# Linear attention on one core: the store of head 13 as three transfers of 76, 48 and 4 partitions

## Chip, cores, metric

One core of one Trainium2 chip runs the kernel. The metric is the device time of one execution in microseconds; before the change it is 171.12 us, the median of three runs (171.07, 171.12, 171.43).

## What is computed

For each of 32 heads, with q, k and v of 2048 x 128 in bf16 and φ(x) = x + 1 for x > 0, exp(x) otherwise:

```python
def reference(q, k, v):
    phi_q = jnp.where(q > 0, q + 1, jnp.exp(q)) + 1e-6
    phi_k = jnp.where(k > 0, k + 1, jnp.exp(k)) + 1e-6
    kv = jnp.einsum("bhsd,bhse->bhde", phi_k, v)
    z = jnp.einsum("bhsd->bhd", phi_k)
    num = jnp.einsum("bhqd,bhde->bhqe", phi_q, kv)
    den = jnp.einsum("bhqd,bhd->bhq", phi_q, z)[..., None] + 1e-6
    return num / den
```

So each head loads three tensors of 512 KB and stores one of 512 KB; 64 MB move in all.

## The kernel before

The work of a head is laid out as 128 partitions (p) by 16 tiles (j) of 128 columns. Row p of a head's tensor in HBM, as `rows` (L228) takes it, is the 16 x 128 elements that belong to partition p: 4 KB without a gap. A load or store of a head is one transfer of 128 such rows.

Per head: SP loads k, q and v (L281). φ is taken as min(exp(x), 1) + 1e-6 plus max(x, 0), in two parts that TensorE adds up. ACT makes exp(k) (L289), DVE min and add (L295), POOL the max (L291) and, for five of 16 tiles, the sum of the two (L300). PE multiplies both with v into kvz_ps (L316), with a column for z (L319). PE transposes q (L335), ACT and DVE make φ of it (L346, L349, L352, L355). PE multiplies φ(q) with kv and z (L370, L371); DVE adds 1e-6 to the denominators (L415), inverts them (L419) and multiplies into o_sb (L391, L397). For the last three heads ACT takes a part of that (L406). SP stores o_sb (L431).

The order is written out by hand. `Plan` (L20) collects every operation with its engine and a due key; each engine's stream is its operations sorted by key. `Plan.emit` (L60) finds which semaphore values each operation has to wait for (L111, L112) and issues it (L113). At the end of SP's stream stand waits for every store's semaphore (L121).

Buffers: six for each of k, v and q (NBI, L158), ten for o_sb (NBO, L159). A load of head h has key h - 6.8 to h - 7.95, so loads run about six heads ahead. A store of head h has key h + 1 + 0.18 h (`late`, L435): the later the head, the further behind its computation the store is issued, so that loads go first, and the stores that are left follow when the last load has been issued. Store 13 has key 16.34, and follows the load of v for head 23. All of these, save the load of v for head 0 (ACT, L276), are issued by SP, in one queue. The semaphores of the stores are one for each o_sb buffer, and three more for the pieces in which the stores of heads 30 and 31 go out (PIECES and EXTRA, L181, L182): two and three groups of tiles, each over all 128 partitions.

Of the kernel before, what the change touches and what calls it, by code (L numbers as in the profile page):

```python
# [144 lines left out]
def bass_standalone__linear_attn_elu__prompt_kernel(  # L145
# [8 lines left out]
    NT = 16  # L154
# [3 lines left out]
    NBI = 6  # L158
    NBO = 10  # L159
# [20 lines left out]

    PIECES = {NH - 2: ((0, 6), (6, NT)), NH - 1: ((0, 6), (6, 12), (12, NT))}  # L181
    EXTRA = {NH - 2: 0, NH - 1: 1}  # L182

    qf = q.rearrange("b h s d -> (b h) s d")
    kf = k.rearrange("b h s d -> (b h) s d")
    vf = v.rearrange("b h s d -> (b h) s d")
    of = out.rearrange("b h s d -> (b h) s d")

    with ExitStack() as es:
        def sb(name, shape, dt):  # L190
            return es.enter_context(nc.sbuf_tensor(name, shape, dt))
# [14 lines left out]
        o_sb = sb("o_sb", [P, NBO, NT, D], bf16)  # L206
# [11 lines left out]
        def dma_sem(name):  # L218
            return dsems[name]

        for n, c in (("k", NBI), ("q", NBI), ("v", NBI), ("o", NBO + 3), ("x", 1)):
            for i in range(c):
                dsems[(n, i)] = es.enter_context(nc.semaphore(f"s_{n}{i}"))

        block = es.enter_context(nc.Block())
        pl = Plan()

        def rows(x, h):  # L228
            return x[h].rearrange("(p j) d -> p (j d)", j=NT)
# [7 lines left out]
               reads=[("id0",)], writes=[("ident",)])  # L237
# [29 lines left out]
        for h in range(NH):  # L267
# [3 lines left out]
            bi, b2, b3, bo = h % NBI, h % 2, h % 3, h % NBO  # L271

            def load(name, buf, src, key, h=h, bi=bi):
# [4 lines left out]
                if name == "v":  # L278
# [11 lines left out]
                   reads=[("k", bi)], writes=[("ek", b2)])  # L290
            pl.add("pool", h, lambda g, bi=bi, b3=b3: g.tensor_scalar(rk_sb[:, b3, :], k_sb[:, bi, :], BIG, 0.0,  # L291
                                                                      op0=ALU.min, op1=ALU.max),
                   reads=[("k", bi)] + ([("emq", 1)] if h == 2 else []), writes=[("rk", b3), ("rkx", b3), ("phik", b3)])
            pl.add("dve", at("emk", -3 + 0.95),
                   lambda d, b2=b2, b3=b3: d.tensor_scalar(emk_sb[:, b3, :], ek_sb[:, b2, :], 1.0, EPS, op0=ALU.min, op1=ALU.add),  # L295
                   reads=[("ek", b2)], writes=[("emk", b3)])

            def added(x, b3=b3):
# [3 lines left out]
                reads=[("emk", b3), ("rkx", b3)] + ([("emq", (h - 1) % 3)] if h else []), writes=[("phik", b3)])  # L302

            def kv(pe, tiles, srcs, h=h, bi=bi, b3=b3):
                for j in tiles:
# [17 lines left out]
                   reads=[("emk", b3), ("rk", b3), ("v", bi), ("ones",), ("vones",)], writes=[("bankkv",)])  # L323
            pl.add("pe", at("kv", -1.2), lambda pe, kv=kv: kv(pe, ADD, (rk_sb,)), reads=[("phik", b3), ("v", bi)], writes=[("bankkv",)])
            pl.add("act", at("kvs", -0.95), lambda a, b3=b3: a.activation(kvs_sb[:, b3, 1:], kvz_ps[:, 1:NC], ACT.Copy),
                   reads=[("bankkv",)], writes=[("kvs", b3)])
            pl.add("dve", at("zs", -1 + 0.905), lambda d, b3=b3: d.tensor_scalar(  # L327
                kvs_sb[:, b3, 0:1], kvz_ps[:, 0:1], kvz_ps[:, NC:NC + 1], None, op0=ALU.add),
                   reads=[("bankkv",)], writes=[("zs", b3)])
# [14 lines left out]
            for half in (0, 1):  # L344
                pl.add("act", h - 1.1 + 0.05 * half,
                       lambda a, b2=b2, c=cols(half): a.activation(eq_sb[:, b2, c], xT_ps[:, c], ACT.Exp),  # L346
                       reads=[("bankx", half)], writes=[("eq", b2, half)])
            pl.add("act", h - 1.0,
                   lambda a, b3=b3, c=cols(1): a.activation(rq_sb[:, b3, c], xT_ps[:, c], ACT.Relu),  # L349
                   reads=[("bankx", 1)], writes=[("rq", b3, 1)])  # L350
            pl.add("dve", at("rq", -2 + 0.948),
                   lambda d, b3=b3, c=cols(0): d.tensor_scalar(rq_sb[:, b3, c], xT_ps[:, c], 0.0, None, op0=ALU.max),  # L352
                   reads=[("bankx", 0)], writes=[("rq", b3, 0)])
            pl.add("dve", at("emq", -2 + 0.955),
                   lambda d, b2=b2, b3=b3: d.tensor_scalar(emq_sb[:, b3, :], eq_sb[:, b2, :], 1.0, EPS, op0=ALU.min, op1=ALU.add),  # L355
                   reads=[("eq", b2, 0), ("eq", b2, 1)], writes=[("emq", b3)])
# [4 lines left out]
            def nbank(b, h=h):  # L361
                return ("bankx", b) if h == NH - 1 and b < 2 else ("banko", b)
# [48 lines left out]
            for g, (b0, b1, place_d, runs) in enumerate(groups):  # L411
# [6 lines left out]
                    reads=banks, writes=[("den", b3, g)])  # L418
                pl.add("dve", key + 0.01, lambda d, b3=b3, b0=b0, b1=b1: d.reciprocal(  # L419
                    rden_sb[:, b3, 4 * b0:4 * b1], den_sb[:, b3, 4 * b0:4 * b1]),  # L420
                    reads=[("den", b3, g)], writes=[("rden", b3, g)])
                if g == 0:
                    pl.add("dve", h + 0.911, last_tile, reads=[nbank(0), nbank(1), ("rden", b3, 0)], writes=[("o", bo, NT - 1)])
                for n, (eng, t0, t1, *place_a) in enumerate(runs):
                    pl.add(eng, h + place_a[0] if eng == "act" else key + 0.012 + 0.004 * n,
                           div_act(t0, t1) if eng == "act" else div(t0, t1),
                           reads=[nbank(b) for b in range(t0 // 3, (t1 + 2) // 3)] + [("rden", b3, g)],
                           writes=[("o", bo, t) for t in range(t0, t1)])

            def store(t0, t1, key, slot, h=h, bo=bo):  # L430
                pl.add("sp", key, lambda sp: sp.dma_start(rows(of, h)[:, t0 * D:t1 * D],  # L431
                                                          o_sb[:, bo, t0:t1].rearrange("p j d -> p (j d)")),
                       reads=[("o", bo, t) for t in range(t0, t1)], dma=("o", slot))

            late = h + 1.0 + 0.18 * h  # L435
            for n, (t0, t1) in enumerate(PIECES.get(h, ((0, NT),))):
                store(t0, t1, late + 0.01 * n, bo if n == 0 else NBO + EXTRA[h] + n - 1)

# [29 lines left out]
```

## Time and profile before

| | |
|---|---|
| time, median of 3 | 171.12 us |
| profiled execution | 171.33 us |
| its span, first to last instruction | 169.5 us |
| mean granted TensorE clock | 0.988 |
| busy PE / PEld / DVE / ACT / POOL | 93% / 92% / 89% / 93% / 62% |
| HBM read / written | 50.33 MB / 16.78 MB, 396 GB/s over the span |

How to read the profile. The page gives the busy share of each engine, then the span in 40 slices, each digit a share in tenths. The row "DMA" is the mean busy share of the core's 16 DMA engines, and the lines on queues give packets, MB and their share of the 16 engines' time: q1 is the queue that SP feeds, q10 that of ACT, q8 and q14 fetch instructions. The chain of work follows the computing instruction that ended last back through what released it. The same DMA rows can be asked for any stretch of the span, again in 40 slices. A line on the issues of one source line gives the time from issue to landing. Behind that stand the landing marks: each transfer raises its semaphore in 16 steps, and the trace has the time of each; a transfer has landed with its last.

The tail of the span, in numbers: the last load is issued at 141.14 us, the last store at 164.41; DVE's last instruction starts at 163.04.

### The profile page before, as it was taken

What the parts mean: (1) busy time and instruction counts of PE and PEld (TensorE: products, weight loads), DVE (VectorE), ACT (ScalarE), POOL (GpSimd) and SP (SyncE); (2) the same over time, 40 slices, a digit from 0 to 9 for tenths busy, and PEclk for the clock granted to TensorE, in tenths of its full rate; (3) what the DMA queues carried; (4) which work ended last, traced back from release to release, by engine and by line L of the source; (5) the groups of instructions that cost most, each with busy time, mean ns of one, the idle gap of its engine ahead of it and who ended that gap; (6) DMA issues with size and microseconds to landing.
All of it is one profiled execution on the core that took longest, in us unless ns stands there. A gap on an engine that the chain in (4) does not pass through costs nothing.

```text
span 169.5 us, 7127 instructions
## 1 busy us (share of the span) xinstructions
PE 157.0 (93%) x3116; PEld 155.6 (92%) x3116; DVE 150.1 (89%) x293; ACT 157.5 (93%) x180; POOL 105.6 (62%) x72
## 2 busy tenths in 40 slices
PE   7559999999999999999999999999999999999920
PEld 7559999999999999999999999999999999999820
DVE  0164999999999999999999999999999999999860
ACT  4699999999999999999999999999999999996950
POOL 3837776666666777666666777666666677755000
PEclk9999999999999999999999999999999999999995
DMA  5999999999999999999999999999999999999984
GB/s 209 407 416 410 412 408 403 399 406 414 414 405 410 417 411 411 414 411 411 410 414 412 410 414 412 409 423 407 413 418 408 409 416 412 410 418 412 411 344 174
DMA packets 22862, 67.56 MB, mean 399 GB/s; under 512 B 2096, under 2 KB 2608, under 8 KB 22832
## 3 DMA queue, kind: packets, MB, share of 16 engines
q1 hardware_dynamic: 22688, 66.59, 98.6%
q8 instruction: 24, 0.39, 0.9%
q10 hardware_dynamic: 144, 0.52, 0.8%
q14 instruction: 6, 0.05, 0.1%
HBM read 50.33 MB, written 16.78 MB: 396 GB/s over the span
## 4 chain that ended last, share of the span: by engine, by line
PE 87%; DMA 3%; DVE 3%; ACT 3%; issue 0%; SPq 0%
PE kvz_ps L316 36%; PE o_ps L370 17%; PE o_ps L371 17%; PE x_ps L335 16%; DMA q_sb<-in_q_dram 3%; DVE o_sb L397 1%; ACT eq_sb L346 1%; PE kvz_ps L319 1%; ACT ek_sb L289 1%; ACT rq_sb L349 1%; DVE emk_sb L295 0%; DVE rden_sb L419 0%; DVE den_sb L415 0%; SPq L281 0%; DVE o_sb L391 0%
## 5 line engine op out<-in xcount | busy, mean ns | idle before, releaser
L300 POOL TENSOR_TENSOR rk_sb<-rk_sb,emk_sb 128x640 bf16<-128x640 bf16 x32 | 44.7, 1398 | 47.3 <-DVE emq_sb L355 41.6
L346 ACT ACTIVATE eq_sb<-x_ps 128x1024 bf16<-128x1024 bf16 x64 | 70.1, 1276 | 3.2 <-PE x_ps L335 3.1
L289 ACT ACTIVATE ek_sb<-k_sb 128x2048 bf16<-128x2048 bf16 x32 | 70.1, 2190 | 1.8 <-DMA k_sb<-in_k_dram 1.8
L397 DVE TENSOR_TENSOR o_sb<-o_ps,rden_sb 128x768 bf16<-128x768 f32 (+2 forms) x63 | 68.0, 1120 | 0.1
L316 PE MATMUL kvz_ps<-v_sb,rk_sb 128*128 128x128 bf16 (+1 forms) x512 | 67.2, 218 | 0.0
L291 POOL TENSOR_SCALAR rk_sb<-k_sb 128x2048 bf16<-128x2048 bf16 x32 | 60.6, 1895 | 2.7 <-DMA k_sb<-in_k_dram 2.0
L370 PE MATMUL o_ps<-kvs_sb,emq_sb 128*128 128x129 bf16 (+1 forms) x536 | 61.1, 217 | 0.3 <-DVE o_sb L397 0.3
L371 PE MATMUL o_ps<-kvs_sb,rq_sb 128*128 128x129 bf16 (+1 forms) x536 | 61.1, 217 | 0.0
L316 PE MATMUL kvz_ps<-v_sb,emk_sb 128*128 128x128 bf16 (+1 forms) x352 | 54.9, 218 | 2.3 <-DVE kvs_sb L327 2.1
L319 PE MATMUL kvz_ps<-ones_sb,rk_sb 128*128 128x1 bf16 x388 | 53.1, 165 | 0.0
L370 PEld LDWEIGHTS o_ps<-kvs_sb,emq_sb 128*128 128x128 bf16 x536 | 50.6, 98 | 0.6 <-DVE o_sb L397 0.4
L371 PEld LDWEIGHTS o_ps<-kvs_sb,rq_sb 128*128 128x128 bf16 x536 | 50.1, 97 | 0.0
L316 PEld LDWEIGHTS kvz_ps<-v_sb,rk_sb 128*128 128x128 bf16 x512 | 46.8, 97 | 0.0
L349 ACT ACTIVATE rq_sb<-x_ps 128x1024 bf16<-128x1024 bf16 x32 | 41.2, 1289 | 0.0
L319 PE MATMUL kvz_ps<-ones_sb,emk_sb 128*128 128x1 bf16 x228 | 37.6, 166 | 0.0
L316 PEld LDWEIGHTS kvz_ps<-v_sb,emk_sb 128*128 128x128 bf16 x352 | 33.5, 97 | 2.8 <-issue 2.4
L335 PE MATMUL x_ps<-ident,q_sb 128*128 128x128 bf16 x512 | 33.8, 219 | 1.7 <-DMA q_sb<-in_q_dram 1.7
L319 PEld LDWEIGHTS kvz_ps<-ones_sb,rk_sb 128*128 128x128 bf16 x388 | 35.4, 96 | 0.0
L335 PEld LDWEIGHTS x_ps<-ident,q_sb 128*128 128x128 bf16 x512 | 29.9, 98 | 2.0 <-DMA q_sb<-in_q_dram 2.0
L295 DVE TENSOR_SCALAR emk_sb<-ek_sb 128x2048 bf16<-128x2048 bf16 x32 | 21.9, 686 | 8.3 <-ACT ek_sb L289 8.3
L352 DVE TENSOR_SCALAR rq_sb<-x_ps 128x1024 bf16<-128x1024 bf16 x32 | 21.9, 683 | 2.0 <-ACT eq_sb L346 2.0
L355 DVE TENSOR_SCALAR emq_sb<-eq_sb 128x2048 bf16<-128x2048 bf16 x32 | 22.8, 712 | 0.4 <-ACT eq_sb L346 0.4
(28 smaller groups left out, 90.8 us busy)
## 6 DMA issues: line engine op xcount, KB each, us to landing
k_sb<-in_k_dram SPq DMA_DIRECT2D x32, 512.0 KB, 13.2
q_sb<-in_q_dram SPq DMA_DIRECT2D x32, 512.0 KB, 13.2
v_sb<-in_v_dram SPq DMA_DIRECT2D x31, 512.0 KB, 13.7
out_dram<-o_sb SPq DMA_DIRECT2D x30, 512.0 KB, 13.7
out_dram<-o_sb SPq DMA_DIRECT2D x3, 192.0 KB, 5.2
v_sb<-in_v_dram ACTq DMA_DIRECT2D x1, 512.0 KB, 4.3
out_dram<-o_sb SPq DMA_DIRECT2D x1, 320.0 KB, 6.1
out_dram<-o_sb SPq DMA_DIRECT2D x1, 128.0 KB, 4.6
```

Of the source, the lines that this page charges most:

```text
L289: lambda a, bi=bi, b2=b2: a.activation(ek_sb[:, b2, :], k_sb[:, bi, :], ACT.Exp),
L291: pl.add("pool", h, lambda g, bi=bi, b3=b3: g.tensor_scalar(rk_sb[:, b3, :], k_sb[:, bi, :], BIG, 0.0, op0=ALU.min, op1=ALU.max), reads=[( ...
L300: pl.add("pool", h + 0.5, lambda g, added=added: g.tensor_tensor(out=added(rk_sb), in0=added(rk_sb), in1=added(emk_sb), op=ALU.add), reads ...
L316: last = pe.matmul(kvz_ps[:, 1 - l:NC + r], lhsT=w, rhs=rhs, start=first, stop=fin, skip_group_check=True)
L319: last = pe.matmul(kvz_ps[:, z:z + 1], lhsT=w, rhs=ones_sb[:, 0:1], start=False, stop=fin, skip_group_check=True)
L335: last = pe.transpose(xT_ps[:, j * P:(j + 1) * P], q_sb[:, bi, j * P:(j + 1) * P], ident[:])
L346: lambda a, b2=b2, c=cols(half): a.activation(eq_sb[:, b2, c], xT_ps[:, c], ACT.Exp),
L349: lambda a, b3=b3, c=cols(1): a.activation(rq_sb[:, b3, c], xT_ps[:, c], ACT.Relu),
L355: lambda d, b2=b2, b3=b3: d.tensor_scalar(emq_sb[:, b3, :], eq_sb[:, b2, :], 1.0, EPS, op0=ALU.min, op1=ALU.add),
L370: pe.matmul(o_ap, lhsT=emq_sb[:, b3, t * P:(t + 1) * P], rhs=kvs_sb[:, b3, c0:c1], start=True, stop=False)
L371: return pe.matmul(o_ap, lhsT=rq_sb[:, b3, t * P:(t + 1) * P], rhs=kvs_sb[:, b3, c0:c1], start=False, stop=True)
L397: return lambda d: d.tensor_tensor(out=o_sb[:, bo, t0:t1, :].rearrange("p (a b) d -> p a b d", b=n), in0=_ap(nfull(b), 512 * b + NC * (t0 ...
```

## The change

The store of head 13 no longer goes out as one transfer of 128 partitions of 4 KB, but as three: partitions 0 to 75, 76 to 123 and 124 to 127, each with all 16 tiles. They take the place of the one store in SP's order, at keys 16.34, 16.35 and 16.36. The first keeps the semaphore of its o_sb buffer; the other two get semaphores of their own, for which two are added. Nothing else is changed: no other transfer, no computation, no buffer.

```diff
     EXTRA = {NH - 2: 0, NH - 1: 1}
+    UNEVEN = 13
...
-        for n, c in (("k", NBI), ("q", NBI), ("v", NBI), ("o", NBO + 3), ("x", 1)):
+        for n, c in (("k", NBI), ("q", NBI), ("v", NBI), ("o", NBO + 5), ("x", 1)):
...
             late = h + 1.0 + 0.18 * h
+
+
+            if h == UNEVEN:
+                r0 = 0
+                for n, r in enumerate((76, 48, 4)):
+                    pl.add("sp", late + 0.01 * n, lambda sp, h=h, bo=bo, r0=r0, r=r: sp.dma_start(
+                        rows(of, h)[r0:r0 + r, :], o_sb[r0:r0 + r, bo].rearrange("p j d -> p (j d)")),
+                        reads=[("o", bo, t) for t in range(NT)], dma=("o", bo if n == 0 else NBO + 2 + n))
+                    r0 += r
+                continue
             for n, (t0, t1) in enumerate(PIECES.get(h, ((0, NT),))):
```

## Prediction

> **What bounds the kernel now.** I read the page from the top: the engines' shares, the slices, the DMA queues, the chain.
>
> ```profile
> DMA  5999999999999999999999999999999999999984
> ...
> q1 hardware_dynamic: 22688, 66.59, 98.6%
> ...
> q8 instruction: 24, 0.39, 0.9%
> ...
> PE 87%; DMA 3%; DVE 3%; ACT 3%; issue 0%; SPq 0%
> ```
>
> The chain says PE, 87%. But it follows computing instructions only, and the last of these, L397 of head 31, starts at 163.04 and takes 0.96 us, so it ends at 164.0, while the span is 169.5. The other lines say what fills those 5.5 us: the 16 DMA engines are full from the second slice to the end, nearly all of it queue q1, which SP feeds. So I ask for the DMA view of the last 4.2 us (165.3 to 169.5, 40 slices of 0.105 us), and for SP's waits:
>
> ```profile
> DMA  9799866555655565556566566422110000000000
> ...
> q1 hardware_dynamic: 505, 0.71, 44.9%
> ```
>
> ```profile
> SPq L121 <- DMA out_dram<-o_sb: 3.9, 5, 1.2
> ```
>
> All 16 engines work until about 165.9. From 166.0 to 167.8 the row stays at 5 to 6 tenths: about 9 of 16 engines work and 7 have nothing left. The last row moves near 168.4. SP's last instructions (L121) wait 3.9 us for just these landings. **The end is set by the nine engines that are behind, not by the sum of the traffic.**
>
> The landing marks say the same. Every transfer leaves 16, one per engine (131 transfers, 2096 marks). The first and the last of one transfer lie 0.5 us apart at 11 us, 2.2 at 40, 3.7 at 80, 5.1 from 119 on. For store 28 (landing 160.03 to 165.12) six engines land within 0.76 us of the first, a seventh 2.2 us after it, the other nine 4.4 to 5.1 after it. What holds an engine back is visible: the 24 instruction packets of q8, 16 KB each, are 0.9% of 16 x 169.5 us = 24.4 us, or 1.0 us of one engine each. The gaps between landing marks show eight engines hit three times each (24 in all), every hit costing 1.3 to 1.6 us, and a ninth falling back slowly. The seven others never meet one. The last store is issued at 164.41; its idle engines land at 166.1 to 166.3, its last mark comes at 169.0. Store 13 is issued at 103.25 and needs 13.8 us to land, with the queue full:
>
> ```profile
> L431 SPq DMA_DIRECT2D out_dram<-o_sb x1: 873/873/873, 103.3 to 103.3; - x1
> ...
> DMA to landing us min/median/max: 13.8/13.8/13.8
> ```
>
> **The change part by part.**
>
> *The shares.* One row of one store is 4 KB. A 128-row transfer is 8 rows on each of 16 engines. Successive marks of one engine lie 1.245 us apart for such a transfer, so a row costs 0.156 us (413 GB/s in the stretch 120 to 140 us, over 16, gives 0.159). The trace shows no other row count. If the shares stay equal, as in all 131 transfers, 48 rows are 3 on each of 16; 76 = 4 x 19 can be dealt equally to 4, 2 or 1 engines at most; 4 rows to 4. I take four: it uses the most engines that equal shares allow, so it is nearest to the row seen. Then four engines carry 19 + 3 + 1 = 23 rows in place of 8, if the 4-row piece goes to the same four: **15 more, +2.34 us**. The other twelve carry 3 in place of 8: **5 fewer, -0.78 us**. The bounds: uneven shares on all 16 change nothing; one engine for all 76 gets 76 + 3 to 4 - 8, about 71.5 rows, or +11.1 us.
>
> *Which four.* No packet record names its engine. If all four are among the seven that finish early: the nine finish 0.78 us earlier, with 5.08 - 0.78 = 4.30 us behind the first. Of the four, an engine that was up to 0.76 behind comes to 3.10, under 4.30. The seventh, 2.22 behind, would come to 2.22 + 2.34 = 4.56 and would then be last: 4.56 - 5.08 = **-0.52 us**. Without it the gain is the whole **-0.78 us**. By count, four out of seven include it 4 times in 7. So -0.52 is the likelier of the two.
>
> For the four being early ones I have one hint. Packets of one engine follow each other at 155 ns, exact to 1 ns over long stretches, so engines can be followed by their phase. Records that start in the same nanosecond keep the order of the table they came from. Of 776 such pairs 619 fit one order of the engines, in which four of the early seven stand ahead of every engine that fetches (one against two of these: 29 to 0 and 21 to 0). Two more early ones stand in the middle, one at the very end. Whether that table runs by number, or as text does (0, 1, 10, 11, ..., 15, 2, 3, ...), the numbers 0 to 3 fall on early engines. It is a hint, since 157 pairs do not fit.
>
> *Page and row.* On the four, the Trainium skill ("DMA: Bandwidth & Descriptors", section "Why a DMA increments its semaphore by 16 and not by 1") says that a transfer from SP uses the largest count up to 16 that divides the rows, on the lowest-numbered engines: 76 on four, 48 on 16, 4 on four. No run here shows this; it would give the same +15 and -5 rows on engines 0 to 3. Against the change speaks the same page's section "Rules for kernel authors": coalesce small transfers, use one 128-partition transfer. With the page's fixed cost of about 2 us per transfer (a fit for another issuing path) two more would be +4 us if nothing hid them, 175.1; the row of 13.8 us to landing, some ten transfers deep, says they are hidden.
>
> *Two more issues on SP.* The 35 issues of L431 take 0.33 to 3.22 us, median 1.08, most of it waiting for room in the queue. Two more cost 0.66 to 2.2 us of SP. Behind them wait the load of k for head 25 (issued 104.22, 13 us before it lands) and all later ones. About 13 us of rows lie ahead of every engine, so none runs dry: nothing. Without that cover it would be the 0.66 to 2.2 us. The three pieces wait for the same writers of o_sb as the one store did, and DVE's next write into that buffer, of head 23, comes at about 127 us (head 26's L397 starts at 141.16, less three heads of 4.75); store 13 landed at 117.06, so 2.34 us more is in time. Two more end waits at L121 are 28 ns each, on stores long landed: 0 to 0.06 us.
>
> *Loads.* They also land when the latest engine does, and PE has no slack for that near head 28. The chain, PE's transposes:
>
> ```profile
> 135.60 0.89 PE x_ps L335 x16
> ...
> 140.39 0.89 PE x_ps L335 x16
> 141.28 0.13 issue
> 141.41 0.33 PE kvz_ps L316 x3
> ...
> 145.41 0.89 PE x_ps L335 x16
> ...
> 150.16 0.89 PE x_ps L335 x16
> ```
>
> The steps are 4.79, 5.02 and 4.75 us, where the usual one is 4.73: about 0.35 us lost, v of head 28 landing at 141.32, just ahead of the kvz matmul at 141.41. With the nine earlier, part of that goes. It buys nothing at the end: the nine work through a full queue, whenever the last stores are issued.
>
> **Sum.** Profiled execution 171.33 us (span 169.5 and 1.8 around it): 171.33 - 0.52 = 170.81. The median of the runs, 171.12, is 0.21 under it, so **170.6 us**; with -0.78, 170.3.
>
> **Rivals.**
> - *The gain is whole (-0.78):* the seventh engine isn't among the four. 170.3. For it: 3 in 7 by count.
> - *A late engine is among the four:* slower. An engine more than 5.08 - 2.34 = 2.74 us behind becomes the last one and sets the end. All nine are past that point, at 4.4 to 5.1, so the end moves by +1.6 to +2.34: 172.8 to 173.5. Loads are as late; PE's last work at 164 moves up to 2.3 us, to 166.3, and stays hidden behind the queue. For it: nine of 16 are late, and four taken blindly would nearly always include one. Against it: the order of equal starts.
> - *Shares stay even:* 76 rows as 4 or 5 on each of 16: 171.1, no change. Against it: no transfer seen has uneven shares.
> - *All 76 rows on one engine:* +11.1 on that engine, less up to 5.1 of lead: +6.0 to +11.1, 177 to 182. Against it: every transfer seen spreads as widely as its rows allow.
>
> **How the numbers follow.** -0.52: 0.47. -0.78: 0.30. Even shares: 0.07. A late engine among the four: 0.13. One engine: 0.03. A measurement of this kernel can tell 0.2%, 0.34 us, from no change; the first two are past that. Faster 0.77, same 0.07, slower 0.16. The range 170.0 to 171.4 takes in the first three, 0.84, with some 0.3 us for the scatter of the runs (171.07 to 171.43) on either side.
>
> **What would show it.** In the last 4.2 us the stretch at 5 to 6 tenths is 0.8 us shorter; with -0.52 it ends in some slices where one engine works alone. The 76-row piece lands without the nine, 9 to 13 us after its issue. First and last landing mark of the loads after it lie about 4.3 us apart, not 5.1, or less if the first engines were among the four. PE's step at head 28 falls towards 4.74. Wrong: landing spread of 6.7 to 7.4 us after store 13 (a late engine among the four), or the spread unchanged (even shares).

## The result and the profile after

| | before | after |
|---|---|---|
| median (10 runs each, in one comparison) | 171.37 us | 170.84 us |
| lowest and highest | 171.06, 171.61 | 170.72, 171.01 |
| profiled execution | 171.33 us | 170.80 us |
| its span | 169.5 us | 168.9 us |
| busy PE / DVE / ACT | 93% / 89% / 93% | 93% / 89% / 93% |

The ratio is 0.9974, 95% interval 0.9963 to 0.9985: the change makes the kernel faster, by 0.45 us (0.26 to 0.63) by the ratio, 0.53 by the medians. The forecast was -0.52 us, 170.81 us for the profiled execution and 170.6 for the median.

The page of the changed kernel, the same lines as before. A line of code stands one number further down in the changed kernel: the loads are L282, the stores L432, the transposes L336, and the three pieces of store 13 are L442.

```profile
DMA  5999999999999999999999999999999999999995
...
q1 hardware_dynamic: 22696, 66.59, 98.7%
...
q8 instruction: 24, 0.39, 0.9%
...
PE 87%; DMA 3%; DVE 3%; ACT 3%; issue 0%; SPq 0%
```

Nothing here tells the two kernels apart: the same bytes, the same fetches, the same chain on PE. q1 has 8 packets more. All of the difference lies in the end. The DMA view of the same stretch as before, 165.3 to 169.5 us from the span's start, 0.105 us a slice, and SP's waits at the end:

```profile
DMA  9999787878868666755321010000000000000000
GB/s 395 380 385 346 302 322 293 302 293 298 317 220 307 239 229 244 249 180 190 127 73 68 34 54 29 20 20 0 0 0 0 0 0 0 0 0 0 0 0 0
...
q1 hardware_dynamic: 456, 0.62, 39.7%
```

```profile
SPq L121 <- DMA out_dram<-o_sb: 3.5, 4, 1.1
```

Before, the row stood at 5 to 6 tenths until 167.8. Now it stands at 6 to 8 until 167.1, since four of the engines that had been done early now work as well, then it falls off, and the last three slices that move anything show 29, 20 and 20 GB/s. One engine, at 4 KB in 0.156 us, moves 26 GB/s: the last 0.3 us belong to one engine. The last landing mark comes at 168.47 us; before, it came at 168.99. That difference, 0.52 us, is the whole gain of the profiled execution.

The marks also say why the latest engine alone sets this end. In all 13 traces of this study, those of the experiments below too, the last mark of the program comes 3.80 to 3.88 us after the last mark of store 28, the fourth store from the end, although the end itself lies anywhere from 167.26 to 170.06 us. Stores 29 to 31 bring each engine the bytes of 24 more rows, 3.74 us at 0.156: the engine that is last at store 28 works on with hardly a gap and sets the end.

The three pieces on SP, and what stands behind them (start, duration, instruction):

```profile
103.10 2.29 SPq L442 DMA_DIRECT2D out_dram<-o_sb  x3
105.48 0.37 SPq L282 DMA_DIRECT2D k_sb<-in_k_dram  x1
```

The load of k for head 25 is issued 1.26 us later than before (104.22) and lands 0.34 us earlier (117.95 rather than 118.29): the later issue is covered by the queue.

PE's transposes from the chain of waits:

```profile
135.77 0.89 PE x_ps L336 x16
...
140.49 0.89 PE x_ps L336 x16
...
145.22 0.89 PE x_ps L336 x16
...
149.97 0.89 PE x_ps L336 x16
```

The steps are 4.72, 4.73 and 4.75 us; the 5.02 at head 28 is gone. v of head 28 lands at 140.50 rather than 141.32, ahead of its first kvz matmul at 141.22. The change is not the only thing that removes this step, though: in the trace of the experiment with even shares v of head 28 lands at 141.32, as before the change, PE comes to it at 141.48 by itself, and the steps are 4.72 and 4.73 as well. The last store is issued at 164.21 rather than 164.41, and this 0.2 us earlier start is not what ends the run: the engine that is last works through a full queue until then.

**How many engines, and which.** The landing marks of the three pieces, leaving out a first step that comes right after an issue (103.83 and 105.55 here): the 76-row piece has four (114.03, 114.55, 114.77, 115.62), the 48-row piece 16, the 4-row piece four (114.69, 115.20, 115.41, 116.27). The second four follow the first four by 0.65 us each, which is 3 rows of the 48-row piece and one of the 4-row piece (4 x 0.156 = 0.62) on the same engine. The offsets of the four among each other, 0, 0.52, 0.74 and 1.59, fit four engines that were ahead just before: in the load of v for head 23, the transfer ahead of store 13, the seven earliest marks lie 0, 0.01, 0.07, 0.29, 0.52, 0.73 and 1.60 us behind the first. The last of them is the seventh early engine. The counts agree with the Trainium skill ("DMA: Bandwidth & Descriptors", section "Why a DMA increments its semaphore by 16 and not by 1"), which gives 4, 16 and 4 engines, counted from the lowest number; the marks carry no engine numbers, so that part is not shown here.

### The profile page after: what moved, and what is told of

Read it like the earlier page. It is cut to its first block, busy times and chain, and to the rows that moved or that the text cites. A ratio compares the mean times of both kernels' runs of the same rounds, so it can differ in the third digit from the quotient of the medians.

```text
span 168.9 us, 7131 instructions
## 1 busy us (share of the span) xinstructions
PE 156.8 (93%) x3116; PEld 155.5 (92%) x3116; DVE 150.0 (89%) x293; ACT 157.4 (93%) x180; POOL 105.5 (62%) x72
## 4 chain that ended last, share of the span: by engine, by line
PE 87%; DMA 3%; DVE 3%; ACT 3%; issue 0%; SPq 0%
PE kvz_ps L317 36%; PE o_ps L371 17%; PE o_ps L372 17%; PE x_ps L336 16%; DMA q_sb<-in_q_dram 3%; DVE o_sb L398 1%; ACT eq_sb L347 1%; PE kvz_ps L320 1%; ACT ek_sb L290 1%; ACT rq_sb L350 1%; DVE emk_sb L296 0%; DVE rden_sb L420 0%; DVE den_sb L416 0%; SPq L282 0%; DVE o_sb L392 0%
## 5 line engine op out<-in xcount | busy, mean ns | idle before, releaser
L347 ACT ACTIVATE eq_sb<-x_ps 128x1024 bf16<-128x1024 bf16 x64 | 68.0, 1208 | 3.2 <-PE x_ps L336 3.2
L290 ACT ACTIVATE ek_sb<-k_sb 128x2048 bf16<-128x2048 bf16 x32 | 67.9, 2122 | 1.7 <-DMA k_sb<-in_k_dram 1.7
L350 ACT ACTIVATE rq_sb<-x_ps 128x1024 bf16<-128x1024 bf16 x32 | 39.2, 1224 | 0.0
L336 PE MATMUL x_ps<-ident,q_sb 128*128 128x128 bf16 x512 | 34.0, 219 | 1.8 <-DMA q_sb<-in_q_dram 1.7
L336 PEld LDWEIGHTS x_ps<-ident,q_sb 128*128 128x128 bf16 x512 | 29.9, 98 | 2.2 <-DMA q_sb<-in_q_dram 2.0
```

Of the source, the lines that this page charges most:

```text
L290: lambda a, bi=bi, b2=b2: a.activation(ek_sb[:, b2, :], k_sb[:, bi, :], ACT.Exp),
L336: last = pe.transpose(xT_ps[:, j * P:(j + 1) * P], q_sb[:, bi, j * P:(j + 1) * P], ident[:])
```

## Experiments

The theory: the end is set by the latest of 16 engines; each carries its own share of rows, at 0.156 us a row, plus its own fetch packets; the change takes 5 rows from the late ones and puts 15 on four early ones. The rivals: three issues, or a later issue order on SP, are what gains; the gain comes through the loads and PE; or something other than the latest engine sets the end. All medians are in us, "before" is a run of the kernel before in the same comparison, and the intervals are of the ratio to it. Where the number of pieces differs, the number of extra semaphores is edited with it, a line that the diffs here do not show.

**Three transfers with even shares.** 64, 48 and 16 rows are 4, 3 and 1 on every engine.

```diff
-                for n, r in enumerate((76, 48, 4)):
+                for n, r in enumerate((64, 48, 16)):
```

> Store 13 as 64, 48 and 16 partitions: three transfers at the same place in SP's order, but 4 + 3 + 1 = 8 rows on each of 16 engines, as before the change. Theory (the end is set by the engine that is furthest behind, and only rows per engine count): no change against before, within 0.1 us. Rival (the gain comes from three issues in place of one, or from their place in SP's order): the same 0.5 us as the change.

Measured: 171.33, before 171.46, ratio 0.9996 (0.998 to 1.0011). No change. Three issues are worth nothing by themselves; the gain needs the uneven shares. PE's step at head 28 is gone in this trace, and the last mark comes at 169.00 (168.99 before): without that step, too, nothing is gained at the end.

**Two transfers of 124 and 4 rows.** All 128 rows go to four engines, 32 each: 24 more there, 8 fewer elsewhere.

```diff
-                for n, r in enumerate((76, 48, 4)):
+                for n, r in enumerate((124, 4)):
```

> Store 13 as 124 and 4 partitions: 31 + 1 = 32 rows on the four engines, 24 more than before, none on the other twelve, 8 fewer. Theory: the nine late engines gain 8 x 0.156 = 1.24 us, but the seventh engine, 2.22 us behind the first at the end, gets 24 x 0.156 = 3.73 us and comes to 5.96 against 5.08: 0.9 us slower than before. Rival (every row taken off the nine late engines is a gain): 1.2 us faster.

Measured: 172.39, before 171.46, ratio 1.0064 (1.0049 to 1.0078): +1.1 us by the ratio, +0.93 by the medians. Both pieces have four landing marks. The DMA view from 165.3 to 170.5 us, 0.13 us a slice:

```profile
DMA  9999999988763332121110000000000000000000
GB/s 358 382 386 425 382 394 378 362 303 303 284 244 122 130 138 87 67 83 67 51 47 20 20 24 24 35 24 24 24 24 20 24 24 8 0 0 0 0 0 0
```

From slice 22 on the row shows 20 to 35 GB/s for 12 slices, 1.6 us: a single engine is left, the seventh, while the 15 others are done. Too much on an early engine makes it the latest.

**The same change on store 25.**

```diff
-    UNEVEN = 13
+    UNEVEN = 25
```

> The same 76, 48 and 4 partitions, but for the store of head 25, which is issued after the last load. Theory (total rows per engine up to the end): 0.5 us faster than before, as at head 13. Rival (the gain comes from loads that land earlier, so that PE does not wait at head 28): no change, since no load is behind this store; PE's late step at head 28 is then still there.

Measured: 171.01, before 171.46, ratio 0.9981 (0.9967 to 0.9996): -0.33 us by the ratio, -0.45 by the medians. It still gains where every load has been issued before it (the last at 140.65, this store at 147.03), so the gain needs no load that lands earlier. The interval holds -0.5 as well as -0.1, so it does not tell whether a place so late keeps all of it. The trace kept is of a run of 171.40 us, which gained nothing:

```profile
DMA  8998797899987666423211000000000000000000
GB/s 346 376 351 332 283 371 283 303 332 395 385 288 293 224 249 224 161 107 122 102 68 49 15 29 29 15 29 29 15 29 20 29 0 0 0 0 0 0 0 0
```

In these 4.2 us (165.3 to 169.5) one engine is alone for the last ten slices; its last mark comes at 169.03, the next engine's at 168.02. By its place in the marks it is the seventh early engine, 5.89 us behind the first at store 28, where the trace of the change has 5.37. So the 15 others were done 0.97 us ahead of the end of the kernel before (168.99), and in this run the seventh took the gain back. Why it is 0.5 us further behind here isn't shown.

**112, 10, 3, 2 and 1 rows.** This numbers the engines: if a piece of r rows up to 16 goes to the first r engines, the marks of one piece that are missing in the next belong to known numbers.

```diff
-                for n, r in enumerate((76, 48, 4)):
+                for n, r in enumerate((112, 10, 3, 2, 1)):
```

> Store 13 as 112, 10, 3, 2 and 1 partitions. If a transfer uses the largest number of engines up to 16 that divides its rows: 7 rows on all 16, one more on engines 0 to 9, one more on 0 to 2, on 0 and 1, on 0; so 3, 2 and 1 rows more than before on three early engines, and none more on a late one. Theory: no change in time, within 0.15 us, and the landing marks of the small pieces tell which engine is how far behind. Rival (each further transfer costs the queue about what an issue costs SP): four more issues, 1.3 us or more, slower.

Measured: 171.21, before 171.46, ratio 0.9994 (0.998 to 1.0007). Five transfers in place of one cost nothing that can be seen here. The Trainium skill's rule to coalesce (same page, section "Rules for kernel authors") therefore has no price in this place, where the queue is some ten transfers deep. The pieces leave 10, 3, 2 and 1 marks after their issue steps. The single row's mark, 112.78, is engine 0; the two-row piece adds 113.40 (engine 1), the three-row piece 112.97 (engine 2). In the ten-row piece 113.89 is the seventh early engine, 115.11 to 115.34 are four late ones, and of 112.21, 112.23 and 112.35 one is engine 0 and two are further early ones. That fits the order which the prediction had read from equal starts: 0 to 3 early, then late ones, two early ones at the places 8 and 9. Why 4 to 7 should be those four follows from that order, not from these marks alone.

**The change again.**

```diff
(the kernel of the change, nothing edited)
```

> The change itself once more (76, 48 and 4 partitions), to stand on the same chip beside the next ones. Every theory: 0.5 us faster than before.

Measured: 170.96, before 171.39, ratio 0.9973 (0.9961 to 0.9986).

**The fourth engine spared.** 69, 48, 4, 4 and 3 rows: engines 0 to 2 carry 29 rows, the fourth 5, the others 3.

```diff
-                for n, r in enumerate((76, 48, 4)):
+                for n, r in enumerate((69, 48, 4, 4, 3)):
```

> Store 13 as 69, 48, 4, 4 and 3 partitions: by the marks of the run with 112, 10, 3, 2 and 1 these are 23 rows on each of engines 0 to 2, 3 on all 16, two more on 0 to 3 and one more on 0 to 2. So 29 rows on engines 0 to 2 (21 more than before), 5 on engine 3, the seventh one (3 fewer), 3 on the rest (5 fewer). Theory (the seventh engine held the change to 0.52 us): the limit is now the nine late ones less 5 rows, 0.78 us faster than before, 0.26 faster than the change; the last marks come from several engines together, not from one alone. Rival (5 rows off the late engines do not bring more than the change showed, or five transfers cost something): 0.5 us faster or less.

Measured: 170.85, before 171.39, ratio 0.9964 (0.9951 to 0.9977), -0.62 us. Its interval holds the -0.78 near its edge, and the change's -0.45 too. The trace kept is of a run of 171.11 us, the slowest of the twelve; its last mark comes at 168.77, with another engine at 168.76, only 0.22 us before that of the kernel before. So it was run again:

> The store of head 13 as 69, 48, 4, 4 and 3 partitions once more (29 rows on engines 0 to 2, 5 on the fourth, 3 on the others). Theory: the fourth engine, which is 2.2 us behind, no longer sets the end, the latest engines with 5 rows fewer do, 0.78 us under before. Rival (the other engines' lag varies, and five issues or the last packets take 0.2 back): 0.5 to 0.6 under before, as the first time, no better than the change.

Measured: 170.72, before 171.40, ratio 0.9958 (0.9944 to 0.9973), -0.72 us. Its trace is of a run of 170.57 us; the last mark comes at 168.23, 0.76 us before that of the kernel before. The DMA view from 165.3 to 169.5:

```profile
DMA  9999997787688766654422110000000000000000
```

The row falls off in steps, with several engines finishing close together, not one alone. The mean of its two ratios is 0.9961, that of the change's two is 0.9974 (0.9974 and 0.9973): 0.2 us between them, of the size expected (0.78 - 0.52 = 0.26), but with overlapping intervals. As measured it is the fastest kernel of the study that computes everything; that it beats the change is likely, not settled.

**A late engine loaded.** 88 and 40 rows: 11 engines take 8 rows each, then ten of them 4 more.

```diff
-                for n, r in enumerate((76, 48, 4)):
+                for n, r in enumerate((88, 40)):
```

> Store 13 as 88 and 40 partitions: by the same rule 8 rows on each of engines 0 to 10 and 4 on each of 0 to 9, so 12 rows (4 more than before) on engines 0 to 9, 8 on engine 10, none on 11 to 15. Engines 4 to 7 are late ones. Theory: the latest of all is among 4 to 6, so 4 x 0.156 = 0.62 us slower than before, although five late or middling engines lose 8 rows. Rival (what counts is the number of engines that a store keeps busy, or the mean): no change, the bytes are the same.

Measured: 171.74, before 171.39, ratio 1.0028 (1.0013 to 1.0043): +0.48 us by the ratio, +0.35 by the medians. The pieces have 11 and 10 marks. Slower, as the theory has it; the expected +0.62 lies inside the interval (0.22 to 0.74). Moving rows is no gain by itself: it depends on whose they become.

**Fewer instruction fetches.** In these three kernels a part of the first contraction is left out on TensorE, so that fewer instructions are fetched; their output is not that of the reference. First, the kernel before with 952 of 3,116 matmuls left out: the products with min(exp(k), 1) of 11 tiles, and the z columns after head 0:

```diff
-                        first, fin = (j == SPLIT[0] and src is emk_sb), j == ADD[-1]
+                        first, fin = j == SPLIT[0], j == ADD[-1]
...
-                        if not l + r:
+                        if h == 0 and not l + r:
...
-            pl.add("pe", at("kv", -1.2), lambda pe, kv=kv: kv(pe, SPLIT, (emk_sb, rk_sb)),
+            pl.add("pe", at("kv", -1.2), lambda pe, kv=kv: kv(pe, SPLIT, (rk_sb,)),
```

> The kernel before, with part of the computation left out: for the 11 tiles that are not added up, PE leaves out the products with min(exp(k), 1), and for heads after the first the column products that make z for most tiles. That is 952 of 3116 matmuls with their weight loads, 1904 of 6232 PE instructions; all transfers stay as before. Theory (the nine engines are late because PE's instructions are fetched through eight of them): 16 or 17 instruction packets of 16 KB in place of 24, two hits on each engine in place of three, the last stores' first and last mark 3.5 to 3.9 us apart in place of 5.1, and 1.2 to 1.6 us faster, all of it at the tail of the queue. Rival (the engines are late for another reason that goes with time or with the traffic): the spread stays at about 5 us, and the time within 0.3 us, since the traffic is the same.

Measured: 171.46, before 171.39, ratio 0.9997 (0.9982 to 1.0013). No change, where -1.2 to -1.6 was expected. PE's busy time before, then PE's busy time and the fetches from this kernel's page:

```profile
PE 157.0 (93%) x3116; PEld 155.6 (92%) x3116; DVE 150.1 (89%) x293; ACT 157.5 (93%) x180; POOL 105.6 (62%) x72
```

```profile
PE 138.0 (81%) x2164; PEld 123.3 (73%) x2164; DVE 148.8 (88%) x293; ACT 157.3 (93%) x180; POOL 105.5 (62%) x72
...
q8 instruction: 17, 0.28, 0.6%
```

That 19 us less of PE work gain nothing speaks against PE as the bound, whatever the chain says. For the fetches it was a miss, with a reason in the trace: 17 packets on eight engines are two each and one more. In the marks of the last load (149.0 to 152.9 us) the engines lie up to 3.9 us apart, as expected, and the seventh early one at 1.4. But at store 28 one engine is 5.3 us behind the first, as far as the latest before (5.1), and the next 3.9. The seventeenth packet starts at 158.6 us, between the two. The DMA view from 165.3 to 169.5:

```profile
DMA  6667646656655322211111000000000000000000
GB/s 229 244 268 268 244 181 239 229 200 220 220 185 210 132 88 93 83 59 59 54 44 44 29 29 15 29 29 15 29 29 29 20 20 29 10 0 0 0 0 0
```

Thirteen slices at 10 to 29 GB/s, 1.4 us: one engine. Followed back through its marks, it is set back at about 16.6, 86.0 and 157.9 us; the first, ninth and seventeenth packets start at 16.5, 86.6 and 158.6. So 264 matmuls fewer had to decide between the theory and a rival (the end is set by something else). Four SPLIT and four ADD tiles' rk products less, on top of the edit above:

```diff
-            pl.add("pe", at("kv", -1.2), lambda pe, kv=kv: kv(pe, SPLIT, (rk_sb,)),
+            pl.add("pe", at("kv", -1.2), lambda pe, kv=kv: kv(pe, SPLIT[:7], (rk_sb,)),
...
-            pl.add("pe", at("kv", -1.2), lambda pe, kv=kv: kv(pe, ADD, (rk_sb,)), reads=[("phik", b3), ("v", bi)], writes=[("bankkv",)])
+            pl.add("pe", at("kv", -1.2), lambda pe, kv=kv: kv(pe, ADD[-1:], (rk_sb,)), reads=[("phik", b3), ("v", bi)], writes=[("bankkv",)])
```

> The kernel before, with products of the first contraction left out on TensorE: all those with the emk operand, the z column for heads 1 to 31, and the rk products of four SPLIT tiles and of four ADD tiles (8 of 16 key tiles count; the output is not the reference's). About 1,200 of 3,116 matmuls go, so by the 17 packets of the run with 952 fewer (2,164 matmuls), 15 or 16 fetch packets on q8 are expected: each of the eight engines is hit twice, none thrice. Transfers and stores are those of before. Theory (the end is set by the latest engine, and only fetch packets make engines late): the lags of the last transfer reach 3.9 us rather than 5.1, as those of the engines hit twice did in that run, and the time is 1.2 us less than before, 170.2 by a before of 171.4. Rival (the end is set by something other than the latest engine, and the 0.5 of the change is an accident of order): no change, within 0.2%, as in the run with 952 fewer.

Measured: 170.07, before 171.40, ratio 0.9923 (0.9904 to 0.9941): -1.3 us. Its page and its last 4.2 us (163.5 to 167.7):

```profile
q8 instruction: 15, 0.25, 0.5%
```

```profile
DMA  8997657667666666745664654453322000000000
```

Two packets fewer than in the kernel ahead of it take the lone engine away, and 1.4 us with it (171.46 to 170.07, in two comparisons with equal runs of before). The marks of store 28 lie 3.6 us apart; in the kernel ahead they lie 5.3 apart, before 5.1. An end of computing that comes earlier is not what differs: the last store is issued at 162.3 us in the kernel ahead and at 162.5 here. The rival falls.

**The change on this kernel.** The same diff as the change, on the kernel with 15 fetches.

> The same products left out as in the kernel beside it (8 of 16 key tiles without emk; the output is not the reference's), and the store of head 13 as 76, 48 and 4 partitions. Theory: the latest engines are now only 3.9 us behind the first, but the seventh engine of the first ones is still 2.2 behind, and with 15 rows more (2.34 us) it ends at 4.56; so the same change that was worth -0.5 us now costs 4.56 - 3.87 = +0.7 us against its own base (the kernel beside it), and stands 0.5 us under the kernel before. The stretch at the end has one engine alone, late by 0.7 to 1.5 us behind the next. Rival (three issues or the place of the rows are worth 0.5 by themselves): 0.5 us under the kernel beside it.

Measured: 170.92, before 171.40, ratio 0.9976 (0.996 to 0.9992), and against the kernel with 15 fetches in the same comparison +0.85 us (170.92 - 170.07); +0.7 was expected. The same edit that gains 0.5 us loses 0.85 here. Its last 4.2 us (164.9 to 169.1):

```profile
DMA  7886876765432342200000000000000000000000
GB/s 288 327 312 249 327 297 244 249 219 215 161 132 98 112 156 93 73 24 24 15 29 15 29 29 15 29 29 29 15 29 20 20 10 0 0 0 0 0 0 0
```

From slice 18 to 33 one engine works alone at 10 to 29 GB/s, 1.7 us. In the marks of the last load (v of head 31) the latest engine stands 4.70 us behind the first and the next 3.77; without the change all 16 stand within 3.54.

## Why the prediction was right, and where it was not

- **What bounds the kernel** was right. Uneven shares gain or lose by whose rows they are, even shares change nothing, 19 us of PE work less gain nothing, two fetch packets fewer gain 1.4 us.
- **The shares** were right: 19 + 3 + 1 rows on four engines, 3 on twelve. The first mark of the last load comes 0.77 us earlier than before (148.03, 148.80), for 5 rows (0.78 worked out); the engine that was first of all is now some 3.0 to 3.1 us behind (3.12 worked out, 20 rows' difference).
- **Which four** was right, the seventh among them, so that -0.52 and not -0.78 was the case that came. This was the step with the least under it: that none of the nine late engines is among the four rested on the order of equal starts, a hint, and -0.52 before -0.78 on a count, 4 in 7. The run bears both out; that it was -0.52 was partly luck. The seventh engine stands 4.65 to 4.68 us behind the new first one at the last load, and about 5.37 at the end (2.22 + 2.34 + 0.78 = 5.34 by the prediction's terms). Sparing it gave some 0.2 of the other 0.26 us, with overlapping intervals.
- **Two more issues and the coalesce rule**: nothing, as forecast; five transfers cost nothing either.
- **PE's stall at head 28** went, and bought nothing at the end, as forecast. But it went with even shares and at store 25 too, so it is no sign of the change: whether PE waits there also depends on when PE itself arrives.
- **The base of the sum** was off. The prediction took 0.21 us off the profiled execution because the median of three runs was lower; with 10 runs the median was 171.37. The step that stands is 171.33 - 0.52 = 170.81; measured 170.84. The 170.6 is lower by that 0.2, a scatter of three runs.
- **One sign named in advance was wrong**: the marks of later loads were to lie 4.3 us apart, and "the spread unchanged" was to mean even shares. In the marks of the last load the spread is 5.03 us, and 5.07 before. The step that failed is "4.30 us behind the first", which took the first engine as standing still. Three of the early engines (the ones 0 to 0.3 us behind) are not among the four; they lost the same 5 rows as the late ones and moved with them. The end does not feel this, because the sum counts from the old first engine, but the spread does. The count of marks of each piece would have been the sound sign.
- The piece of 76 rows was to land 9 to 13 us after its issue: its four marks come 10.9 to 12.5 us after it.

Of the experiments' own forecasts, two were clearly off. The kernel with 17 fetches was put at -1.2 to -1.6 and did not change: the fetches were counted rightly, but the theory had treated 17 like 16. The kernel with the fourth engine spared was put at -0.78 and gave -0.62 and -0.72. The last 0.1 is not explained: several engines finish within some tenths there, and any of them that is a little later in one run sets the end.

## What to carry to other kernels

When the DMA queues are full from start to end, look at the last microseconds slice by slice: a share that falls to half and stays there, or a few slices at the rate of one engine, says that a few of the 16 engines set the end, and that bytes moved off these engines are worth their full time while bytes moved onto the idle ones are free up to their lag. How late each engine is depends on things that a small edit moves, such as the number of instructions fetched, so a hand-dealt split like 76, 48 and 4 has to be dealt again after every change: the same split was worth -0.5 us with 24 fetches and +0.85 us with 15. To judge a split, read the landing marks of an early transfer and a late one, engine by engine, and not only first against last.

## What the runs showed of the hardware

- One fetch packet more can cost a kernel over 1 us: 24 packets (three on each of eight engines) and 17 (three on one engine alone) gave the same time within 0.1 us, 15 gave 1.3 us less. A packet takes 0.9 to 1.1 us in q8's records (one took 1.3), and an engine that met one falls 1.3 to 1.6 us behind.
- Beside a first step right after its issue, a transfer from SP's queue left as many marks as the largest count up to 16 that divides its rows: 16 for 48 and 112 rows, 11 for 88, 10 for 40 and 10, 4 for 76, 124 and 4, 3 for 69 and 3, 2 for 2, 1 for 1.
